# First batch of a forgetting-attention + MLP kernel on one core: unread matmuls out of its stream, block copies in halves ahead of the divisions, decay rows later, MLP steps among the last block's scores

## The chip, the cores and the metric

The kernel runs on one core of a Trainium2 chip. The engines of a core work through their own instruction streams and wait for each other by semaphores: PE (TensorE, matmuls; its weight loads are shown as PEld), DVE (VectorE), ACT (ScalarE), POOL (GpSimd) and SP (SyncE); the last two, and ACT, also issue DMAs. The metric is the time of the kernel on the device in microseconds (us); lower is better. Times inside a profile are counted from the start of its span.

## The reference

The inputs are q, k, v of 8 batches x 8 heads x 576 positions x 64, a forget gate f of 8 x 8 x 576, and two weights w_in (512 x 2048) and w_out (2048 x 512). The output is 4608 x 512, float32.

```python
scores = scale * np.matmul(q, k.transpose(0, 1, 3, 2))
log_f = np.log(np.clip(f, 0.0001, 1.0))
cum = np.cumsum(log_f, axis=-1)
decay = cum[:, :, :, None] - cum[:, :, None, :]
scores = np.where(causal, -1000000000.0, scores + decay)
attn = np.exp(scores - max); attn = attn / (sum + 1e-09)
x = matmul(attn, v), heads side by side: 4608 x 512
h = x @ w_in
g = h - np.tanh(h)
out = g @ w_out
```

## The kernel before

**Tiling.** The 576 positions of a head are four blocks of 128 and one of 64. The decay goes into the score matmul itself: next to their 64 channels, q and k carry three more rows (67 in all) that hold the cumulated log gate (as a high part `chi`, a low part `clo`, and `cq` for q) against rows of ones and minus ones. Scores are made transposed, keys on partitions; `exp` on ACT (L272 for the first batch, L329 for the others) writes them to fp16 tiles `e`; a second matmul with v, which carries a column of ones, gives values and row sums in a tile `av`; DVE divides (L285 to L287 for the first batch, L354 to L356 for the others) into `xn`. The divided values are turned into `XR`, a ring of four batches of x, transposed. The MLP runs over units `u` of 512 tokens: `mlp1` makes 128 rows of h for 512 tokens (for unit 0: two such for 256 tokens, L381), ACT takes tanh (L369), DVE adds (L371); `mlp2` multiplies with w_out. One MLP **step** is one `mlp1` tile or a quarter of an `mlp2` tile, about 0.87 us of PE at full clock.

**The order is written out by hand** (`manual_schedule`): every engine runs its instructions in the order of the Python calls, and waits in that order. From batch 1 on, `slot` interleaves one pair of heads (seven score tiles, the values of the pair before, transposes, loads) with a number of MLP steps, `TAKE` for the first six pairs and 8 for the rest. The change doesn't touch this part but for one number in `TAKE`.

**The first batch** is done before that, block by block, so that work can start when the first blocks of q and k have arrived:

- `load_first` and `load_v` (L90, L86) load blocks of q, k and v by POOL, `load_qk` batch 1's q and k, `load_win` w_in in two halves, `load_wout` w_out in four parts. A ring of eight semaphores lets the next load on POOL's queue start when the one eight places before it has landed.
- `decay_sum`, `decay_turn`, `decay_cols` sum the log gate (DVE, L153), transpose it (PE, L172, tile `ct`) and write it into the extra columns of q and k of the first batch (DVE, L177 to L180). `decay_rows` makes `chi`, `cq`, `clo` for all batches (DVE, L158 to L162); `load_aug(1)` puts them into batch 1's `QT` and `KT` by DMAs on SP (L148 to L150).
- `trans0(ib, what, pool, eng)` transposes block `ib` of q or k for all 8 heads (8 matmuls, L252) into one PSUM tile and copies it to `QT` or `KT` in one instruction (DVE L257, ACT L255).
- `scores0(ib, ti)` makes one tile of 512 columns of block `ib`'s scores (L267, with L270 for the mask on the diagonal) and its `exp`. Heads come in order, so a block's first tiles read the first heads alone. There are two PSUM tiles for scores and ten `e` tiles.
- `values0(ib)` makes the values of block `ib` and the division behind them. There is one `av` tile.
- `turn0(ib)` transposes `xn` on PE (L296) and copies it into `XR` (DVE L297).
- `spin(n)` issues n matmuls of ones with ones, 512 columns each (L223), into an `av` tile that nobody reads.

In the order before, a spin of 8 opens PE's stream, and seven more spins stand between the blocks' parts. A block's transposes and copies come after the division of the block two before it, and the first three MLP steps come after `scores0(4, 2)`, `scores0(4, 3)` and `scores0(4, 4)`.

Batch 1's q and k are loaded in another layout and transposed by `trans` (PE L234), whose result is copied in two parts, each by ACT (L241) or DVE (L243) as its last argument says ("AV", "VV").

Of the kernel before, what the change touches and what calls it, by code (L numbers as in the profile page):

```python
# [22 lines left out]
def kernel(  # L23
# [76 lines left out]
    def load_v(b, n):  # L100
        load_block(vn[b % 2], v, b, n)
# [65 lines left out]
    def decay_turn(blocks):  # L167
        if not CT:
            CT.append(ps_tr.tile([P, UW], FP32, tag="tr", name="ct"))
        for ib in blocks:  # L170
            t0 = min(ib * P, S - P)
            nc.tensor.transpose(out=CT[0][:, ib * H:(ib + 1) * H], in_=cum[0:H, t0:t0 + P], identity=id32)  # L172

    def decay_cols(b0, b1):
        ct = CT[0][:, b0 * H:b1 * H].rearrange("p (n h) -> p n h", h=H)
        hi = ka[:, b0:b1, :, D]
        nc.vector.tensor_scalar(out=qa[:, b0:b1, :, D + 2], in0=ct, scalar1=inv_qscale,  # L177
                                scalar2=-SHIFT * inv_qscale, op0=ALU.mult, op1=ALU.add)
        nc.vector.tensor_scalar_mul(out=hi, in0=ct, scalar1=inv_qscale)
        nc.vector.scalar_tensor_tensor(out=ka[:, b0:b1, :, D + 1], in0=ct, scalar=inv_qscale, in1=hi,  # L180
                                       op0=ALU.mult, op1=ALU.subtract)
# [36 lines left out]
    E, XN, GT, M2 = {}, {}, {}, {}  # L218

    def spin(n):  # L220
        av = ps_av.tile([P, 2, 512], FP32, tag="av", name="spin")
        for _ in range(n):
            nc.tensor.matmul(out=av[:, 0, :], lhsT=ones16[:, 0:P], rhs=ones16[:, 0:UW])  # L223

    def trans(b, c, src, dst, eng):
        pn, g3 = S // NT6, NT6 // 2
        if b == 1 and src is kn:
            t32 = ps_m.tile([P, UW], FP32, tag="m", name="t32")
        else:
            t32 = ps_tr.tile([P, UW], FP32, tag="tr", name="t32")  # L230
        t16 = t32.bitcast(FP16)[:, 0:2 * S // 2].rearrange("p (a g n) -> p a g n", a=2, g=g3)
        for a in range(2):
            for g in range(g3):
                nc.tensor.transpose(out=t16[:, a, g, :],  # L234
                                    in_=src[b % 2][:, 2 * c + a, 2 * g:2 * g + 2, :],
                                    identity=id16[0:pn, 0:pn])
        for e in range(2):
            to = dst[b % 2][0:D, 2 * c:2 * c + 2, e:S:2].rearrange("d a (p g) -> d a p g", g=g3)
            of = t16[e * D:(e + 1) * D, :, :, :].rearrange("d a g p -> d a p g")
            if eng[e] == "A":  # L240
                nc.scalar.activation(out=to, in_=of, func=AF.Copy)  # L241
            else:
                nc.vector.tensor_copy(out=to, in_=of)  # L243

    def trans0(ib, what, pool, eng):
        src, dst = (qa, ka)[what], (QT, KT)[what][0]
        p0 = max(0, (ib + 1) * P - S)
        pn = P - p0
        t32 = pool.tile([P, UW], FP32, tag="tr" if pool is ps_tr else "m", name="t32")
        t16 = t32.bitcast(FP16)[0:D + 3, 0:H * pn].rearrange("p (h n) -> p h n", h=H)  # L250
        for h in range(H):
            nc.tensor.transpose(out=t16[:, h, :], in_=src[p0:P, ib, h, 0:D + 3], identity=id16[p0:P, p0:P])  # L252
        to = dst[:, :, ib * P:ib * P + pn]
        if eng == "A":
            nc.scalar.activation(out=to, in_=t16, func=AF.Copy)  # L255
        else:
            nc.vector.tensor_copy(out=to, in_=t16)  # L257

    def scores0(ib, ti):
        w = min(P, S - ib * P)  # L260
        n = UW // w
        ps = ps_sc.tile([P, 512], FP32, tag="sc", name="ps")
        e = aex.tile([P, 512], FP16, tag="e", name="e")
        todo = [(h, j) for h in range(H) for j in range(ib + 1)][n * ti:n * ti + n]
        for i, (h, j) in enumerate(todo):
            at = slice(i * w, (i + 1) * w)
            nc.tensor.matmul(out=ps[:, at], lhsT=KT[0][:, h, j * P:(j + 1) * P],  # L267
                             rhs=QT[0][:, h, ib * P:ib * P + w], start=True, stop=(j < ib))
            if j == ib:
                nc.tensor.matmul(out=ps[:, at], lhsT=neg16, rhs=tri16[:, 0:w], start=False, stop=True)  # L270
            E[(0, h, j, ib)] = e[:, at]
        nc.scalar.activation(out=e, in_=ps, func=AF.Exp, scale=qscale)  # L272

    def values0(ib):
        w = min(P, S - ib * P)
        av = ps_av.tile([P, 2, 512], FP32, tag="av", name="av")
# [10 lines left out]
        nc.vector.tensor_tensor(out=XN[(0, ib)].rearrange("p (i c) (a d) -> p i (c a) d", i=2, a=2),  # L287
                                in0=av[:, :, :, 0:D], in1=rs.to_broadcast([w, 2, HH, D]), op=ALU.mult)
# [131 lines left out]
    def step(n=1):  # L420
        for fn, *args in mlp[done[0]:done[0] + n]:
            fn(*args)
        done[0] += n
# [29 lines left out]
        step(take - given)  # L453

    load_v(0, 0)
    spin(8)
    decay_sum(0, 2 * P)
    decay_turn((0, 1))
    decay_cols(0, 1)
    decay_sum(2 * P, S)  # L460
    trans0(0, 0, ps_m, "V")
    trans0(0, 1, ps_m, "A")
    decay_turn((2, 3, 4))
    decay_cols(2, NJ)
    load_first(qa, q, 2)
    load_first(ka, k, 2)
    load_v(0, 1)
    load_first(qa, q, 3)
    load_first(ka, k, 3)
    load_v(0, 2)  # L470
# [6 lines left out]
        load_qk(qn, q, 1, h, h + 2)  # L477
        load_qk(kn, k, 1, h, h + 2)
    load_win(DFF // 2, DFF)
    spin(2)  # L480
    decay_cols(1, 2)
    decay_rows(False)
    trans0(1, 0, ps_m, "V")
    scores0(0, 0)
    scores0(0, 1)
    trans0(1, 1, ps_tr, "V")
    decay_rows(True)
    load_aug(1)
    spin(2)
    scores0(1, 0)  # L490
    values0(0)
    scores0(1, 1)
    spin(1)
    trans0(2, 0, ps_m, "V")
    scores0(1, 2)
    trans0(2, 1, ps_tr, "V")
    scores0(1, 3)
    turn0(0)
    values0(1)
    spin(1)  # L500
    scores0(2, 0)
    scores0(2, 1)
    spin(1)
    trans0(3, 0, ps_m, "V")
    scores0(2, 2)
    turn0(1)
    scores0(2, 3)
    trans0(3, 1, ps_tr, "V")
    for e in EL:
        nc.vector.memset(e, 0.0)  # L510
    nc.vector.memset(KT[1][:, :, S:PITCH], 0.0)
    nc.vector.memset(vn[1][D:P, NJ - 1, :, 0:D], 0.0)
    nc.vector.memset(vn[1][:, :, :, D:VW], 1.0)
    for n in range(NJ):
# [5 lines left out]
    scores0(2, 4)  # L520
    scores0(2, 5)
    scores0(3, 0)
    values0(2)
    scores0(3, 1)
    scores0(3, 2)
    scores0(3, 3)
    turn0(2)
    trans0(4, 0, ps_m, "V")
    scores0(3, 4)
    trans0(4, 1, ps_tr, "V")  # L530
    scores0(3, 5)
    scores0(3, 6)
    scores0(3, 7)
    scores0(4, 0)
    values0(3)
    scores0(4, 1)
    scores0(4, 2)
    step()
    turn0(3)
    scores0(4, 3)  # L540
    step()
    scores0(4, 4)
    step()
    values0(4)
    trans(1, 0, qn, QT, "AV")
    step()
    trans(1, 0, kn, KT, "VV")
    step()
    TAKE = [4, 4, 3, 3, 10, 9]
# [33 lines left out]
```

## Time and profile before

| what | value |
|---|---|
| three runs | 364.15, 364.20, 362.62 us, median 364.15 |
| the profiled execution | 363.46 us, of which its span 361.8 us |
| L407, `mlp2` matmuls on PE | 576 of mean 378 ns, 140.2 us busy |
| L395, `mlp1` matmuls on PE, units 1 to 8 | 576 of mean 355 ns, 125.6 us busy |
| L272, `exp` of the first batch on ACT | 25 of mean 596 ns, 14.1 us busy |
| L223, spins on PE, up to 41 us | 15, 6.0 us busy |
| granted clock of PE, mean | 0.989 |
| DMA, whole span | 38.70 MB, mean 107 GB/s |

A matmul's duration in the rows includes time that it overlaps with its neighbours, so PE's work is better read from the distance of the starts: the eight matmuls of an `mlp1` step start 0.87 us before whatever follows them. In a timeline row, the brackets at the end hold how long the engine was idle before the instruction and what ended that wait. In the page's rows of 40 digits, each digit is the share of a slice of 9 us in tenths.

### The profile page before, as it was taken

How to read it: one execution, taken by the hardware profiler on the slowest of the kernel's cores; microseconds unless marked ns; L12 is line 12 of the kernel's file. 1: busy time of each engine (PE TensorE's matmuls, PEld its weight loads, DVE VectorE, ACT ScalarE, POOL GpSimd, SP SyncE). 2: the span in 40 equal slices, each digit the busy share in tenths (PEclk: the TensorE clock that was granted, in tenths of full speed). 3: DMA queues.
4: the chain of work that ended last, by engine and by line, in shares of the span. 5: the costliest groups of instructions: out<-in, count | busy, mean ns of one | idle time of the engine just before them, and what ended most of it. 6: DMA issues, size and time to landing. Idle time of an engine off the chain costs nothing.

```text
span 361.8 us, 7844 instructions
## 1 busy us (share of the span) xinstructions
PE 348.7 (96%) x2992; PEld 202.3 (56%) x2992; DVE 192.7 (53%) x358; ACT 223.5 (62%) x411; POOL 150.4 (42%) x288
## 2 busy tenths in 40 slices
PE   7789799999999999999999999999999999999995
PEld 3678687555555555555556875555555554444442
DVE  7653798546981478137823683277327612712810
ACT  5475687456765786568656875687568734613621
POOL 8944623256277626763676357642222210000000
PEclk9996999999999999999999999999999999999999
DMA  9999999999579997999699959991220022011002
GB/s 95 144 203 184 205 200 120 99 138 180 70 57 150 143 150 59 156 152 143 56 150 170 142 53 151 160 153 24 81 71 18 18 74 74 2 52 65 2 31 85
DMA packets 148439, 38.70 MB, mean 107 GB/s; under 512 B 137330, under 2 KB 142770, under 8 KB 148402
## 3 DMA queue, kind: packets, MB, share of 16 engines
q0 software_dynamic: 100128, 18.36, 69.3%
q1 hardware_dynamic: 48194, 19.77, 26.8%
q8 instruction: 23, 0.38, 0.4%
q14 instruction: 14, 0.11, 0.1%
q10 hardware_dynamic: 80, 0.08, 0.1%
HBM read 36.85 MB, written 9.44 MB: 128 GB/s over the span
## 4 chain that ended last, share of the span: by engine, by line
PE 91%; DVE 4%; ACT 3%; issue 1%; ACTq 0%
PE ops L407 34%; PE hps L395 30%; PE ps L320 10%; PE av L348 7%; PE hps L381 3%; PE ps L267 2%; PE spin L223 1%; DVE KT L243 1%; PE av L280 1%; PE t L252 1%; DVE gt L371 1%; PE t L234 1%; ACT e L329 1%; ACT th L369 1%; ACT e L272 1%
## 5 line engine op out<-in xcount | busy, mean ns | idle before, releaser
L407 PE MATMUL ops<-wout,gt 128*128 128x512 f16 x576 | 140.2, 378 | 0.0
L371 DVE TENSOR_TENSOR gt<-hps,th 128x512 f16<-128x512 f32 x144 | 99.1, 690 | 61.7 <-ACT th L369 60.9
L329 ACT ACTIVATE e<-ps 128x512 f16<-128x512 f32 x168 | 99.3, 594 | 49.2 <-PE ps L320 39.7
L395 PE MATMUL hps<-XR,win 128*128 128x512 f16 (+1 forms) x576 | 125.6, 355 | 0.2 <-DVE gt L371 0.2
L369 ACT ACTIVATE th<-hps 128x512 f32<-128x512 f32 x144 | 86.1, 598 | 28.8 <-PE hps L395 22.9
L339 POOL TENSOR_SCALAR_AFFINE_SELECT e<-e 128x128 f16<-128x128 f16 x144 | 49.0, 340 | 108.6 <-ACT e L329 108.2
L407 PEld LDWEIGHTS <-gt 128*128 128x128 f16 x576 | 51.8, 97 | 52.8
L395 PEld LDWEIGHTS <-win 128*128 128x128 f16 x576 | 52.3, 97 | 44.3 <-issue 0.5
L320 PE MATMUL ps<-QT,KT 67*128 67x512 f16 (+1 forms) x336 | 70.9, 277 | 3.0 <-DVE KT L243 2.0
L320 PEld LDWEIGHTS <-KT 67*128 67x128 f16 x336 | 32.8, 98 | 35.7 <-DVE KT L243 2.4
L411 ACT ACTIVATE ost<-ops 128x512 f32<-128x512 f32 x36 | 21.5, 598 | 39.2 <-PE ops L407 39.2
L354 DVE TENSOR_SCALAR rs<-av 128x10 f32<-128x10 f32 x28 | 4.6, 164 | 68.3 <-PE av L348 68.2
L86 POOL DMA_DIRECT2D vn<-in_v_dram x40 | 34.3, 859 | 13.1 <-DMA win<-in_moe_w_in_dram 5.1
L348 PEld LDWEIGHTS <-e 128*128 128x128 f16 x784 | 28.1, 97 | 5.5
L348 PE MATMUL av<-vn,e 128*128 128x65 f16 x784 | 29.1, 193 | 0.0
L86 POOL DMA_DIRECT2D qn<-in_q_dram x25 | 21.2, 850 | 9.8 <-PE t L234 3.6
L356 DVE TENSOR_TENSOR xn<-av,rs 128x640 f16<-128x640 f32 x28 | 23.1, 825 | 1.0
L86 POOL DMA_DIRECT2D kn<-in_k_dram x25 | 21.4, 855 | 1.4 <-issue 1.2
L272 ACT ACTIVATE e<-ps 128x512 f16<-128x512 f32 x25 | 14.1, 596 | 10.2 <-PE ps L270 5.4
L381 PE MATMUL hps<-XR,win 128*128 128x256 f16 x128 | 17.4, 281 | 0.0
L243 DVE COPY KT<-t 64x576 f16<-64x576 f16 x16 | 12.7, 796 | 1.9 <-PE t L234 1.8
L243 DVE COPY QT<-t 64x576 f16<-64x576 f16 x12 | 9.6, 803 | 7.5 <-PE t L234 5.2
(78 smaller groups left out, 210.6 us busy)
## 6 DMA issues: line engine op xcount, KB each, us to landing
out_dram<-ost SPq DMA_DIRECT2D x36, 256.0 KB
vn<-in_v_dram POOLq DMA_DIRECT2D x32, 128.0 KB, 5.2
qn<-in_q_dram POOLq DMA_DIRECT2D x24, 128.0 KB, 3.9
kn<-in_k_dram POOLq DMA_DIRECT2D x24, 128.0 KB, 4.1
win<-in_moe_w_in_dram POOLq DMA_DIRECT2D x2, 1024.0 KB, 12.9
wout<-in_moe_w_out_dram POOLq DMA_DIRECT2D x4, 512.0 KB, 12.2
XR<-xn SPq DMA_TRANSPOSE x56
qn<-in_q_dram POOLq DMA_DIRECT2D x1, 576.0 KB, 15.5
```

What stands on the lines that cost most here:

```text
L86: nc.gpsimd.dma_start(out=dst[0:pn, n, h0:h1, 0:D], in_=src[b, h0:h1, n * P:n * P + pn, :].rearrange("h p d -> p h d"))
L243: nc.vector.tensor_copy(out=to, in_=of)
L320: nc.tensor.matmul(out=ps[:, col:col + n], lhsT=KT[b % 2][0:D + 3, h, j * P:(j + 1) * P], rhs=QT[b % 2][0:D + 3, h, i0:i0 + n], start=True ...
L329: nc.scalar.activation(out=e[:, lo:hi], in_=ps[:, lo:hi], func=AF.Exp, scale=qscale)
L339: nc.gpsimd.affine_select(out=view, in_=view, compare_op=ALU.is_ge, fill=0.0, base=0, pattern=pat, channel_multiplier=-1)
L348: nc.tensor.matmul(out=av[:, a, ib, :], lhsT=E.pop((b, 2 * c + a, j, ib)), rhs=vn[b % 2][:, j, 2 * c + a, 0:D + 1], start=(j == 0), stop=( ...
L356: nc.vector.tensor_tensor(out=xn.rearrange("p i (a d) -> p a i d", a=2), in0=av[:, :, :, 0:D], in1=rs.to_broadcast([P, 2, NJ, D]), op=ALU. ...
L369: nc.scalar.activation(out=th, in_=hps, func=AF.Tanh, scale=-1.0)
L371: nc.vector.tensor_tensor(out=gt, in0=hps, in1=th, op=ALU.add)
L381: nc.tensor.matmul(out=hps[:, w * SB:(w + 1) * SB], lhsT=win[:, ci, ft * P:(ft + 1) * P], rhs=XR[:, ci, t * SB:(t + 1) * SB], start=(ci == ...
L395: nc.tensor.matmul(out=hps[:, o:o + n], lhsT=win[:, ci, s * P:(s + 1) * P], rhs=XR[:, ci, t:t + n], start=(ci == 0), stop=(ci == NCH - 1))
L407: nc.tensor.matmul(out=ops, lhsT=GT[(u, ft, m)], rhs=wout[:, ft, :], start=(ft == 0), stop=(ft == NFT - 1))
```

## The change

All of it is in the first batch. `trans0` is split into the transposes (`trans0`, for a range of heads) and the copy (`copy0`, for a range of heads), `values0` into the matmuls and the division (`norm0`), so that they can be ordered apart. `spin` is called with 8 at the start and with 2 behind the first block's transposes, and nowhere else. The rest is order: block 1 and block 2 are copied in halves of four heads; a block's copies are put ahead of the division of the block two before it; `decay_rows` is called between blocks 2 and 3 and between blocks 3 and 4, and `load_aug(1)` after that; v of block 1 is loaded ahead of q and k of block 2; memsets of batch 1's tiles move into the head on DVE, and those of the `el` tiles to POOL; `trans` of batch 1's first k uses ACT for one of its copies; a sixth MLP step is put ahead of the pairs and one is taken out of the second slot.

```diff
-    def trans0(ib, what, pool, eng):
-        src, dst = (qa, ka)[what], (QT, KT)[what][0]
+    T0 = {}
+
+    def trans0(ib, what, pool, h0=0, h1=H):
+        src = (qa, ka)[what]
...
-        to = dst[:, :, ib * P:ib * P + pn]
+    def copy0(ib, what, eng, h0=0, h1=H):
+        w = min(P, S - ib * P)
+        to = (QT, KT)[what][0][:, h0:h1, ib * P:ib * P + w]
         if eng == "A":
-            nc.scalar.activation(out=to, in_=t16, func=AF.Copy)
+            nc.scalar.activation(out=to, in_=T0[(ib, what)][:, h0:h1, :], func=AF.Copy)
         else:
-            nc.vector.tensor_copy(out=to, in_=t16)
+            nc.vector.tensor_copy(out=to, in_=T0[(ib, what)][:, h0:h1, :])
...
+        AV[ib] = av
+
+    def norm0(ib):
+        w = min(P, S - ib * P)
+        av = AV.pop(ib)
```

The order after, in full from the first load to the pairs:

```python
    load_v(0, 0)
    load_v(0, 1)
    spin(8)
    decay_sum(0, 2 * P)
    decay_turn((0, 1))
    nc.vector.memset(KT[1][:, :, S:PITCH], 0.0)
    nc.vector.memset(vn[1][D:P, NJ - 1, :, 0:D], 0.0)
    nc.vector.memset(vn[1][:, :, :, D:VW], 1.0)
    decay_cols(0, 1)
    trans0(0, 0, ps_m)
    trans0(0, 1, ps_m)
    copy0(0, 0, "V")
    copy0(0, 1, "A", 0, HH)
    copy0(0, 1, "A", HH, H)
    spin(2)
    decay_sum(2 * P, S)
    decay_cols(1, 2)
    scores0(0, 0)
    scores0(0, 1)
    decay_turn((2, 3, 4))
    for h in (0, HH):
        trans0(1, 0, ps_m, h, h + HH)
        trans0(1, 1, ps_m, h, h + HH)
    copy0(1, 0, "V", 0, HH)
    copy0(1, 1, "V", 0, HH)
    decay_cols(2, NJ)
    ...
    copy0(1, 0, "V", HH, H)
    copy0(1, 1, "V", HH, H)
    scores0(1, 0)
    scores0(1, 1)
    values0(0)
    trans0(2, 0, ps_m)
    scores0(1, 2)
    trans0(2, 1, ps_tr)
    scores0(1, 3)
    for h in (0, HH):
        copy0(2, 0, "V", h, h + HH)
        copy0(2, 1, "V", h, h + HH)
    scores0(2, 0)
    scores0(2, 1)
    norm0(0)
    trans0(3, 0, ps_m)
    copy0(3, 0, "V")
    scores0(2, 2)
    trans0(3, 1, ps_tr)
    copy0(3, 1, "V")
    scores0(2, 3)
    values0(1)
    norm0(1)
    scores0(2, 4)
    turn0(0)
    decay_rows(False)
    scores0(2, 5)
    scores0(3, 0)
    scores0(3, 1)
    trans0(4, 0, ps_m)
    copy0(4, 0, "V")
    scores0(3, 2)
    trans0(4, 1, ps_tr)
    copy0(4, 1, "V")
    scores0(3, 3)
    values0(2)
    norm0(2)
    scores0(3, 4)
    turn0(1)
    decay_rows(True)
    load_aug(1)
    load_v(1, 0)
    load_v(1, 1)
    for e in EL:
        nc.gpsimd.memset(e, 0.0)
    ...
    scores0(3, 5)
    scores0(3, 6)
    scores0(3, 7)
    scores0(4, 0)
    scores0(4, 1)
    values0(3)
    norm0(3)
    turn0(2)
    scores0(4, 2)
    step()
    scores0(4, 3)
    step()
    scores0(4, 4)
    turn0(3)
    step()
    values0(4)
    norm0(4)
    trans(1, 0, qn, QT, "AV")
    step()
    trans(1, 0, kn, KT, "AV")
    step()
    step()
    TAKE = [4, 3, 3, 3, 10, 9]
```

What the two lines of "..." leave out are loads in the order of before: q and k of blocks 2 and 3, v of blocks 2 and 3, q, k, v of block 4, the first half of w_in, batch 1's q and k of heads 0 to 3, the second half of w_in; and then v of batch 1's blocks 2 to 4, q and k of its heads 4 to 7, and w_out. The same part of the order before:

```python
    spin(2)
    decay_cols(1, 2)
    decay_rows(False)
    trans0(1, 0, ps_m, "V")
    scores0(0, 0)
    scores0(0, 1)
    trans0(1, 1, ps_tr, "V")
    decay_rows(True)
    load_aug(1)
    spin(2)
    scores0(1, 0)
    values0(0)
    scores0(1, 1)
    spin(1)
    trans0(2, 0, ps_m, "V")
    scores0(1, 2)
    trans0(2, 1, ps_tr, "V")
    scores0(1, 3)
    turn0(0)
    values0(1)
    spin(1)
    scores0(2, 0)
    scores0(2, 1)
    spin(1)
    trans0(3, 0, ps_m, "V")
    ...
    step()
    trans(1, 0, kn, KT, "VV")
    step()
    TAKE = [4, 4, 3, 3, 10, 9]
```

More of the change, by code (lines that the diff above doesn't have):

```diff
@@ L216 @@
                     LOADS.setdefault((p0 + 3, 2 * n + a), []).append(lambda b=b, dst=dst, src=src, a=a, c=c: place(dst, src, b, a, c))
-    E, XN, GT, M2 = {}, {}, {}, {}
+    E, XN, GT, M2, AV = {}, {}, {}, {}, {}
     def spin(n):
@@ L243, in trans @@
                 nc.vector.tensor_copy(out=to, in_=of)
-    def trans0(ib, what, pool, eng):
-        src, dst = (qa, ka)[what], (QT, KT)[what][0]
+    T0 = {}
+    def trans0(ib, what, pool, h0=0, h1=H):
+        src = (qa, ka)[what]
         p0 = max(0, (ib + 1) * P - S)
         pn = P - p0
[L249 to L252, printed above, removed]
-        to = dst[:, :, ib * P:ib * P + pn]
+        if (ib, what) not in T0:
+            t32 = pool.tile([P, UW], FP32, tag="tr" if pool is ps_tr else "m", name="t32")
+            T0[(ib, what)] = t32.bitcast(FP16)[0:D + 3, 0:H * pn].rearrange("p (h n) -> p h n", h=H)
+        for h in range(h0, h1):
+            nc.tensor.transpose(out=T0[(ib, what)][:, h, :], in_=src[p0:P, ib, h, 0:D + 3],
+                                identity=id16[p0:P, p0:P])
+    def copy0(ib, what, eng, h0=0, h1=H):
+        w = min(P, S - ib * P)
+        to = (QT, KT)[what][0][:, h0:h1, ib * P:ib * P + w]
         if eng == "A":
-            nc.scalar.activation(out=to, in_=t16, func=AF.Copy)
+            nc.scalar.activation(out=to, in_=T0[(ib, what)][:, h0:h1, :], func=AF.Copy)
         else:
-            nc.vector.tensor_copy(out=to, in_=t16)
+            nc.vector.tensor_copy(out=to, in_=T0[(ib, what)][:, h0:h1, :])
     def scores0(ib, ti):
@@ L455 @@
     load_v(0, 0)
+    load_v(0, 1)
     spin(8)
@@ L458 @@
     decay_turn((0, 1))
+    nc.vector.memset(KT[1][:, :, S:PITCH], 0.0)
+    nc.vector.memset(vn[1][D:P, NJ - 1, :, 0:D], 0.0)
+    nc.vector.memset(vn[1][:, :, :, D:VW], 1.0)
     decay_cols(0, 1)
+    trans0(0, 0, ps_m)
[3 more added lines that the diff above has]
+    copy0(0, 1, "A", HH, H)
+    spin(2)
     decay_sum(2 * P, S)
-    trans0(0, 0, ps_m, "V")
-    trans0(0, 1, ps_m, "A")
+    decay_cols(1, 2)
+    scores0(0, 0)
+    scores0(0, 1)
     decay_turn((2, 3, 4))
+    for h in (0, HH):
[3 more added lines that the diff above has]
+    copy0(1, 1, "V", 0, HH)
     decay_cols(2, NJ)
@@ L466 @@
     load_first(ka, k, 2)
-    load_v(0, 1)
     load_first(qa, q, 3)
@@ L479 @@
     load_win(DFF // 2, DFF)
-    spin(2)
-    decay_cols(1, 2)
-    decay_rows(False)
[L483 to L486, printed above, removed]
+    copy0(1, 0, "V", HH, H)
+    copy0(1, 1, "V", HH, H)
+    scores0(1, 0)
+    scores0(1, 1)
+    values0(0)
+    trans0(2, 0, ps_m)
+    scores0(1, 2)
+    trans0(2, 1, ps_tr)
+    scores0(1, 3)
+    for h in (0, HH):
+        copy0(2, 0, "V", h, h + HH)
+        copy0(2, 1, "V", h, h + HH)
+    scores0(2, 0)
+    scores0(2, 1)
+    norm0(0)
+    trans0(3, 0, ps_m)
+    copy0(3, 0, "V")
+    scores0(2, 2)
+    trans0(3, 1, ps_tr)
+    copy0(3, 1, "V")
+    scores0(2, 3)
+    values0(1)
+    norm0(1)
+    scores0(2, 4)
+    turn0(0)
+    decay_rows(False)
+    scores0(2, 5)
+    scores0(3, 0)
+    scores0(3, 1)
+    trans0(4, 0, ps_m)
+    copy0(4, 0, "V")
+    scores0(3, 2)
+    trans0(4, 1, ps_tr)
+    copy0(4, 1, "V")
+    scores0(3, 3)
+    values0(2)
+    norm0(2)
+    scores0(3, 4)
+    turn0(1)
     decay_rows(True)
     load_aug(1)
[L489 to L508, printed above, removed]
-    for e in EL:
[L510 to L514, printed above, removed]
+    load_v(1, 0)
+    load_v(1, 1)
+    for e in EL:
+        nc.gpsimd.memset(e, 0.0)
+    for n in range(2, NJ):
         load_v(1, n)
@@ L519 @@
         load_wout(t, t + 4)
[L520 to L530, printed above, removed]
     scores0(3, 5)
@@ L534 @@
     scores0(4, 0)
+    scores0(4, 1)
     values0(3)
-    scores0(4, 1)
+    norm0(3)
+    turn0(2)
     scores0(4, 2)
     step()
-    turn0(3)
     scores0(4, 3)
@@ L542 @@
     scores0(4, 4)
+    turn0(3)
     step()
     values0(4)
+    norm0(4)
     trans(1, 0, qn, QT, "AV")
     step()
-    trans(1, 0, kn, KT, "VV")
+    trans(1, 0, kn, KT, "AV")
     step()
-    TAKE = [4, 4, 3, 3, 10, 9]
+    step()
+    TAKE = [4, 3, 3, 3, 10, 9]
     for p in range(NPAIR, len(pairs) + 1):
```

## The prediction

> **What bounds the kernel now.** I read the page first, then its clock row, then the head in equal intervals, then the PE timeline and the DMA landings there.
>
> ```profile
> PE 348.7 (96%) x2992; PEld 202.3 (56%) x2992; DVE 192.7 (53%) x358; ACT 223.5 (62%) x411; POOL 150.4 (42%) x288
> ...
> PE   7789799999999999999999999999999999999995
> PEclk9996999999999999999999999999999999999999
> ```
>
> TensorE (PE) is full from the fifth slice (9 us each) to the end: what follows the head goes on PE's own time, so an edit in the head is worth what it moves the start of that dense stretch. The first four slices are not full, and in the fourth the granted clock is 0.6. The windows, cut at the moments where the clock changes:
>
> ```profile
> 12.20:15.62 3.42, 2.56 (x45) 2.33 (x45) 2.35 (x5) 1.75 (x3) 3.42 (x6) 1.00 2.26 150
> 15.62:19.03 3.41, 2.15 (x31) 1.81 (x32) 1.32 (x5) 1.09 (x2) 3.36 (x7) 1.00 1.49 153
> 19.03:22.44 3.41, 3.11 (x65) 2.92 (x63) 2.61 (x10) 2.79 (x5) 1.73 (x2) 1.00 1.11 201
> 22.44:25.86 3.42, 2.96 (x48) 2.42 (x46) 2.18 (x6) 2.51 (x5) 0.00 (x0) 1.00 1.29 207
> 25.86:29.27 3.41, 3.08 (x53) 2.99 (x51) 0.02 (x1) 1.94 (x4) 3.38 (x5) 0.50 1.13 209
> 29.27:32.68 3.41, 3.41 (x40) 2.88 (x38) 1.12 (x4) 1.68 (x3) 0.41 (x1) 0.50 1.92 172
> 32.68:36.09 3.41, 3.41 (x69) 3.03 (x67) 2.15 (x4) 2.28 (x4) 1.63 (x3) 1.00 1.92 178
> ```
>
> Columns: length, then busy time of PE, weight load, DVE, ACT, POOL, the granted clock, DMA share, GB/s. From 25.86 to 32.68 PE ran at half clock: 6.8 us that held some 3.4 us of full-speed work. The PE timeline has the waits and the first MLP steps:
>
> ```profile
> 13.00 0.39 PE L223 MATMUL spin<-ones 128*128 128x512 f16 x1 [0.88 <-DVE xn L287]
> ...
> 17.18 0.39 PE L223 MATMUL spin<-ones 128*128 128x512 f16 x1 [1.22 <-DVE xn L287]
> ...
> 30.04 1.89 PE L381 MATMUL hps<-XR,win 128*128 128x256 f16 x8
> ...
> 32.69 1.04 PE L381 MATMUL hps<-XR,win 128*128 128x256 f16 x8
> ...
> 40.61 0.39 PE L320 MATMUL ps<-QT,KT 67*128 67x512 f16 x1 [1.96 <-DVE KT L243]
> ```
>
> An unread matmul (spin) writes the tile `av`, so it waits for the division (L287) that reads the tile before, and all of PE stands behind it: 0.88 and 1.22 us. The first MLP step starts at 30.04 (1.7 us long at half clock, against 0.87 later), the second at 32.69. Batch 1's first scores wait 1.96 us for the two KT copies on DVE. PE's waits from 5.4 to 41 us add to 6.0 us (0.29, 0.26, 0.29, 0.88, 1.22, 0.30, 0.46, 0.33, 1.96).
>
> **Arrivals.** Issue plus time to landing, block by block, from the DMA view: q and k of block 2 land at 10.65 and 11.49, of block 3 at 13.64 and 14.53, of block 4 at 17.82 and 18.11; the first half of w_in (issued 14.81, 10.8 us) at 25.61, its second half at 33.06; batch 1's heads 4 to 7 at 39.4 (q) and 41.0 (k); batch 2's q and k at 54.2 and 57.6. The DMA row is full to about 90 us, so I take these as set by the DMA engines. The new order moves v of block 1 ahead of q and k of block 2: these come one place later (11.5 and 12.5, the landings of the next two places before). Every later load keeps its place.
>
> **Part by part.**
>
> Spins: five of the seven behind the first eight go, 5 x 0.216 = 1.1 us of PE, and with them the waits of 0.88 and 1.22.
>
> Head: copies of KT block 0 in two halves on ACT. One copy took 1.02 us (7.22 to 8.24); a half I take at 0.59, as the 512-element exponentials take, so the first four heads' scores can start at 7.8 instead of 8.74. Chi and cq (1.1 us of DVE) no longer precede block 1's copies; with the halves at 0.42 (the 512-element copies of block 4) block 1's first scores start at 10.4 instead of a wait that ended at 11.06. By then PE runs into block 2's arrival at 11.5, so little of this counts by itself. Three memsets (0.27, 0.27, 0.12) move into DVE's 0.83 us wait for `ct`: nothing, or 0.1 us if the wait shrinks.
>
> Blocks 2 to 4: the new order puts both transposes and their copies ahead of the division of two blocks earlier. Laid end to end by hand with the rows' pitches (a 128-column matmul 0.057 us, 8 transposes 0.46 to 0.5, an `av` matmul 0.03, a 1024-element copy 0.61, a half 0.36, a division 1.05, an exponential 0.49 in a row, 0.6 plus about 0.1 when waited for), I get block 2's first scores at 13.5 (17.40 before), block 3's at 17.0 (q, k 3 copied at 16.4), its eight exponentials done at 22.2, values of block 3 at 22.6, and scores0(4, 2) finished at 24.2. Of 17 exponentials between 14.0 and 24.9 that makes 0.64 us each; before, 15 took 10.3 us, 0.69. So the order is no faster than ACT and PE already show. The first MLP step then waits for w_in at 25.61: PE idles up to 1.4 us, which is also the slack for errors of mine. Chi, cq and clo (2.0 us of DVE) now stand among blocks 3 and 4, where DVE has 11 us of work in 13; the aug loads on SP follow at about 22 instead of 8.9 to 12.8 and need some 1 us (8.87 to 9.92 before): 10 us ahead of batch 1's scores. The three `el` memsets go to POOL, in front of a load that waits for w_in (5.1 us idle there): hidden; without that cover three POOL memsets delay that load by three times the 0.1 us of POOL's own small ones, or up to 0.35 for the three on DVE.
>
> MLP steps: step 1 at 25.65, scores0(4, 3) 0.37, step 2 at about 26.9. Before, step 2 started at 32.69, and the order from there to batch 1 is the same work. That is **-5.8 us**, half of it the half-clock stretch that step 1 no longer falls into.
>
> The 1.96 us gap: KT's second copy goes to ACT (0.80 beside 0.80) and a third step (0.87) is put before batch 1's scores, so I leave 0.3: **-1.7 us**. That step is taken out of a later slot, so it is cover and no gain.
>
> What is late next: all that follows would run 7.5 us earlier against loads that do not move. Batch 1's k heads 4 to 7 are first read at 51.13 - 7.5 = 43.6, after 41.0: fine. Batch 2's q is read at 61.13 - 7.5 = 53.6 (lands 54.2), k at 63.96 - 7.5 = 56.5 (lands 57.6): PE stalls about **+1.1 us**. For my hand schedule slipping past its slack I add **+0.5**.
>
> Sum: 363.46 (profiled execution, 361.8 of span and 1.66 around it) - 5.8 - 1.7 + 1.1 + 0.5 = 357.6. The median before is 0.7 above that execution, within a spread of 1.6; I forecast **357.8 us**.
>
> **The clock, the cost that the trace can't settle.** It fell at 25.86 after an interval in which PE was busy 2.96 of 3.42 us, and not after the one at 15.62 with 2.15 of 3.41 and a 1.22 us wait. Busy time does not decide. Adding up columns in the timeline, each weighted by its rows out of 128, transposes too, I get about 4900, 3750, 5140 and 2940 for the four intervals before the fall: the fall follows the poorest. My new order gives some 5400, 4500, 4400 and, with the wait for w_in, 3600 in the same intervals. So I expect the clock to hold, not by much. Bounds: nothing, or 3.4 us for two half-clock intervals of dense work as before.
>
> [...]
>
> **Rivals.**
>
> 1. The same order, but the clock falls around 25.9 as before, for two intervals under dense MLP steps: + 3.4, and batch 2's loads are then no longer late (- 1.1): 357.6 + 2.3 = about 360. For it: the interval from 22.44 stays the poorest. Against: steps fill it where nothing did.
>
> [...]
>
> 3. The change doesn't deliver: some in-order wait that I mislaid (a division in front of a copy, ACT behind a copy) keeps PE from reaching step 1 until about 30, and no clock is gained: only the 1.7 us at KT, less later stalls: 362.5 to 363.5. Against: every operand of step 1 but w_in is made by about 21, PE's own work from 9 to 24.2 is some 14 us by the pitches above, and so it takes 5 us of new waits. For it: those 14 us leave little room for any.
>
> **How the numbers follow.** Forecast 0.50, rival 1 0.26, rival 2 0.09, rival 3 0.15. A measurement of this kernel tells 0.5% (1.8 us): below 362.3 is faster, above 366.0 slower. Forecast, rival 1 and a third of rival 3 are faster: 0.81; the rest of rival 3 and a little of rival 2 same: 0.11; slower 0.08. The range runs from 355.6 (no slip, batch 2's loads a little earlier) through rival 1 and half of rival 3: 362.8.
>
> **What would show it.** Step 1's L393 row (L381 before) near 25.7 with a wait on the w_in DMA ahead of it; the clock in the windows from 12 to 36 at 1.00 (rival 1: 0.50 near 26 to 33; rival 2: 0.50 from before 20); block 2's scores near 13.5; no wait over 0.5 us at batch 1's first scores, at about 34; a new wait of up to 1 us of PE on batch 2's qn and kn loads near 54 to 57. I am wrong if step 1 starts after 28, or if the dense stretch starts early and PE then shows new waits further on that eat it.

## The result, and the profile after

| | median | runs | profiled execution | its span | mean granted clock |
|---|---|---|---|---|---|
| before | 364.17 us | 362.62 to 364.28 (4) | 363.46 us | 361.8 us | 0.989 |
| after | 357.77 us | 357.69 to 358.57 (4) | 358.57 us | 356.9 us | 1.000 |
| after, measured once more | 357.41 us | 357.28 to 357.56 (4) | 357.32 us | 355.6 us | 0.999 |

The change is faster: 0.9839 of the time before, 95% interval 0.9809 to 0.9869; in the second measurement 0.9825, 0.9806 to 0.9843. The forecast was 357.8 us. The two profiled executions of the same kernel differ by 1.3 us, and both are used below: the first is called "after", the other "after again".

The page of after, the lines that answer to those of before:

```profile
PE 346.6 (97%) x2987; PEld 200.9 (56%) x2987; DVE 191.9 (54%) x358; ACT 224.5 (63%) x413; POOL 150.9 (42%) x291
...
PE   7989998999999999999999999999999999999995
PEclk9999999999999999999999999999999999999999
```

PE is 80% busy or more from the second slice on, and the 0.6 of the fourth slice of the clock row is gone. The windows of after, in steps of 3.41 us from the clock's rise at 10.13 (length, busy time of PE, PEld, DVE, ACT and POOL, granted clock, DMA share, GB/s):

```profile
13.54:16.96 3.42, 3.25 (x54) 2.94 (x52) 2.55 (x9) 2.81 (x6) 3.42 (x6) 1.00 2.24 147
16.96:20.37 3.41, 3.11 (x61) 2.76 (x58) 3.26 (x8) 2.91 (x5) 3.15 (x5) 1.00 1.13 196
20.37:23.78 3.41, 3.17 (x68) 2.86 (x67) 2.54 (x7) 2.65 (x6) 1.86 (x5) 1.00 1.19 202
23.78:27.20 3.42, 3.04 (x76) 2.69 (x74) 1.32 (x5) 2.49 (x5) 2.52 (x4) 1.00 1.23 212
27.20:30.61 3.41, 3.41 (x49) 2.96 (x48) 2.39 (x5) 2.77 (x5) 0.67 (x1) 1.00 1.24 202
```

No interval is at 0.50; before, two were, from 25.86 to 32.68. The steps, in the PE timeline of after (start, duration, and in brackets the idle time before it and what ended it):

```profile
15.00 0.51 PE L274 MATMUL ps<-QT,KT 67*128 67x128 f16 x3
...
27.02 1.04 PE L393 MATMUL hps<-XR,win 128*128 128x256 f16 x8
...
28.20 1.04 PE L393 MATMUL hps<-XR,win 128*128 128x256 f16 x8
...
34.84 1.03 PE L393 MATMUL hps<-XR,win 128*128 128x256 f16 x8 [0.46 <-DVE gt L383]
35.71 0.38 PE L332 MATMUL ps<-QT,KT 67*128 67x512 f16 x1
...
38.18 0.19 PE L332 MATMUL ps<-QT,KT 67*128 67x64 f16 x1 [0.28 <-ACT e L341]
...
48.01 0.30 PE L332 MATMUL ps<-QT,KT 67*128 67x320 f16 x1 [0.62 <-ACT e L341]
...
54.75 0.30 PE L332 MATMUL ps<-QT,KT 67*128 67x320 f16 x1 [0.61 <-ACT e L341]
...
57.68 1.03 PE L419 MATMUL ops<-wout,gt 128*128 128x512 f16 x4
```

The rows of before that answer to the last two:

```profile
59.65 0.30 PE L320 MATMUL ps<-QT,KT 67*128 67x320 f16 x1 [0.61 <-ACT e L329]
...
62.58 1.03 PE L407 MATMUL ops<-wout,gt 128*128 128x512 f16 x4
```

Step 2 starts at 28.20 instead of 32.69, 4.49 us earlier, and batch 1's first scores at 35.71 instead of 40.61, 4.90 earlier, with six MLP steps done instead of five. The waits on the division (0.88 and 1.22) and on KT (1.96) are gone; in their place is a wait of 0.46 for `gt`. The rows behind that say what happened further on. Slots 1, 2 and 3 begin with their first scores at 35.71, 42.47 and 49.22, before at 40.61, 47.18 and 54.11. Slot 2 gave up a step of 0.87 us and has no other work for PE in its place: PE waits in it 0.62 us for ACT's exponentials (48.01), and the slot is only 0.18 us shorter than before (6.75 against 6.93). Slot 1 has as many steps as before and a new wait of 0.28 us (38.18): it is 0.19 us longer (6.76 against 6.57). The wait of 0.61 us in slot 3 was there before too, at 59.65. So the first `mlp2` step starts 4.90 us earlier than before (57.68 against 62.58), no more than batch 1's first scores did: the sixth step is not a gain there, and the span ends 4.9 us earlier.

In after again the same rows come earlier:

```profile
25.73 1.04 PE L393 MATMUL hps<-XR,win 128*128 128x256 f16 x8
...
26.91 0.82 PE L393 MATMUL hps<-XR,win 128*128 128x256 f16 x6
```

(The second row is cut by the end of the view.) In all 14 profiles PE starts at half its later pace: the spins of 512 columns start 0.43 us apart at first, and 0.22 us once the clock has risen. In after the clock rose at 10.13 us, in after again at 6.66, in the profile of before at 5.38; the 1.3 us between the two executions are there by block 2's first scores (15.00 and 13.70), and with the early rise step 2 stands at the 26.9 that was forecast.

### The profile page after: what moved, and what is told of

Read it like the earlier page. It is cut to its first block, busy times and chain, and to the rows that moved or that the text cites. A ratio compares the mean times of both kernels' runs of the same rounds, so it can differ in the third digit from the quotient of the medians.

```text
span 356.9 us, 7839 instructions
## 1 busy us (share of the span) xinstructions
PE 346.6 (97%) x2987; PEld 200.9 (56%) x2987; DVE 191.9 (54%) x358; ACT 224.5 (63%) x413; POOL 150.9 (42%) x291
## 4 chain that ended last, share of the span: by engine, by line
PE 92%; ACT 3%; DVE 2%; DMA 1%; issue 1%; ACTq 0%
PE ops L419 35%; PE hps L407 30%; PE ps L332 10%; PE av L360 7%; PE hps L393 3%; PE ps L274 2%; PE t L255 1%; PE av L287 1%; PE t L234 1%; ACT e L279 1%; ACT th L381 1%; ACT e L341 1%; DVE gt L383 1%; DMA lf<-in_f_dram 1%; PE ps L277 1%
## 5 line engine op out<-in xcount | busy, mean ns | idle before, releaser
L341 ACT ACTIVATE e<-ps 128x512 f16<-128x512 f32 x168 | 99.2, 594 | 47.4 <-PE ps L332 40.0
L393 PE MATMUL hps<-XR,win 128*128 128x256 f16 x128 | 16.6, 272 | 0.5 <-DVE gt L383 0.5
L274 PE MATMUL ps<-QT,KT 67*128 67x128 f16 (+1 forms) x120 | 11.6, 214 | 1.5 <-ACT e L279 0.8
```

What stands on the lines that cost most here:

```text
L341: nc.scalar.activation(out=e[:, lo:hi], in_=ps[:, lo:hi], func=AF.Exp, scale=qscale)
L393: nc.tensor.matmul(out=hps[:, w * SB:(w + 1) * SB], lhsT=win[:, ci, ft * P:(ft + 1) * P], rhs=XR[:, ci, t * SB:(t + 1) * SB], start=(ci == ...
```

## The experiments

Three questions: did the clock hold because the stream got denser, or for another reason; which part of the change brought the time; and what the prediction's misses cost. Each kernel was timed against the kernel before on the same chip: medians there 363.95 (19 runs), 363.55 (13) and 363.97 us (7).

### Which of it is the spins, and which the clock

**old_fill**: before, with six unread matmuls more among block 3's scores.

```diff
+    def fill(n):
+        t = ps_m.tile([P, UW], FP32, tag="m", name="fill")
+        for _ in range(n):
+            nc.tensor.matmul(out=t, lhsT=ones16[:, 0:P], rhs=ones16[:, 0:UW])
...
     scores0(3, 1)
+    fill(1)
```

and one more behind each of `scores0(3, 2)` to `scores0(3, 6)`.

> The old order with six more unread matmuls of 512 columns among block 3's scores, in the stretch 22.4 to 25.9 us ahead of the fall of the clock; they write a PSUM tile of the MLP pool that no engine reads, so they wait for no division. Theory that the clock falls after an interval with too few columns: the clock stays at 1.00 from its first rise to 41 us, the first MLP step starts near 28 instead of 30.0, and the time falls by 1.5 to 2.5 us although 1.3 us of PE work is added. [...]

Measured: 362.23 us (361.64 to 363.27, 10 runs), ratio 0.9963 [0.9944, 0.9982]; the profiled execution kept full clock from 7.29 to the end, with step 1 at 29.56 (not near 28, as expected) and step 2 at 30.96. Its clock row:

```profile
PEclk9999999999999999999999999999999999999999
```

More work on the engine that bounds the kernel, six matmuls of 0.216 us, made the kernel 1.7 us shorter. The waits behind the spins and the 1.96 us at KT are still in its timeline. The clock did not hold in every run: five of the ten have a mean clock of 0.998 or 0.999 and took 361.6 to 361.9 us, the other five have 0.993 to 0.995 and took 362.6 to 363.3; where it fell in these is not known. Of the 19 runs of before beside them, two have 0.999 (361.5 us), three 0.994 or 0.995, and fourteen 0.989 or 0.990 (363.7 to 364.2). The fill is the only edit, so the work in the stretch ahead of 25.86 bears on the fall: with the six matmuls five of ten runs have 0.998 or more, without them two of 19. Before's own runs at 0.999 and at 0.989 or 0.990 are some 2 to 3 us apart.

**old_no_spin**: before, without its five later spins.

```diff
     load_aug(1)
-    spin(2)
     scores0(1, 0)
...
     scores0(1, 1)
-    spin(1)
     trans0(2, 0, ps_m, "V")
...
     values0(1)
-    spin(1)
     scores0(2, 0)
     scores0(2, 1)
-    spin(1)
     trans0(3, 0, ps_m, "V")
```

> The old order with the change's spins only (8 at the start and 2 behind block 0's transposes; five later ones gone), nothing else. Theory that the spins cost by their wait for a division: PE's waits of 0.88 and 1.22 us shrink, the stretch to the first MLP step gets up to 2 us shorter, and the time falls by 0.5 to 2 us unless the clock falls more. Rival, that the spins hold the clock: the half clock comes before 20 us and lasts longer than 6.8 us, and the time rises by 1 to 4 us.

Measured: 359.63 us (359.2 to 361.1, 4 runs), ratio 0.9896 [0.9856, 0.9936]. Deleting five matmuls from the old order, with whole copies, early decay rows and the old tail, brings 4.3 us of the change's 6.4, more than twice what was expected. Step 1 starts at 26.04, step 2 at 27.45, and the clock holds near 25.9. It falls later, at the wait for KT, as the windows of old_no_spin show:

```profile
28.72:32.14 3.42, 3.42 (x66) 3.01 (x62) 2.42 (x6) 2.19 (x4) 0.00 (x0) 1.00 1.78 179
32.14:35.55 3.41, 1.44 (x17) 1.03 (x15) 3.24 (x6) 1.30 (x3) 2.58 (x4) 1.00 2.06 175
35.55:38.96 3.41, 3.41 (x22) 2.48 (x21) 1.30 (x2) 1.96 (x4) 2.68 (x4) 0.50 1.29 205
```

The interval with 1.44 us of busy PE holds the wait:

```profile
35.38 0.48 PE L320 MATMUL ps<-QT,KT 67*128 67x512 f16 x1 [1.97 <-DVE KT L243]
```

Here the wait of about 2 us lies whole in one interval, and the interval after it, dense work, runs at half clock. In before the wait of 1.96 us was shared by two intervals (cut at 39.51) and the clock held. So the same wait cost 1.96 us before and more than that here.

**new_spin**: the change, with one spin put back behind each of the divisions of blocks 0 and 1.

```diff
     norm0(0)
+    spin(1)
...
     norm0(1)
+    spin(1)
```

> The new order with one unread matmul into the av tile right behind each of the first two divisions, so that PE waits for these divisions again. Theory that the order is worth its time because PE no longer stands behind a division: PE waits some 0.8 to 1.2 us at each, the first MLP step moves from 27.0 to about 28.5, and the time rises by 1 to 2 us. Rival, that the gain is the clock alone: the time stays within 0.5 us, as the clock stays at 1.00.

Measured: 360.29 us (359.95 to 363.77, 10 runs), ratio 0.9922 [0.9891, 0.9952]: eight runs at 360.0 to 360.4 with a clock near 1.0, two at 363.7 with 0.986. The profiled execution was one of the two; its timeline has the old waits back, one of 0.74 and one of

```profile
19.37 0.39 PE L223 MATMUL spin<-ones 128*128 128x512 f16 x1 [1.22 <-DVE xn L299]
```

and its windows the old fall:

```profile
18.29:21.70 3.41, 2.02 (x26) 1.59 (x26) 2.35 (x6) 1.53 (x4) 2.87 (x6) 1.00 1.12 210
21.70:25.12 3.42, 3.42 (x47) 3.07 (x46) 0.97 (x3) 1.99 (x4) 2.10 (x3) 0.50 1.28 200
```

Two unread matmuls of together 0.43 us cost 2.5 us with their waits (360.3 against 357.8) and 6 us where the clock falls as well (363.7). The price of a spin here is not its length but the division it waits for.

### Which of it is the tail, and which the order

**old_nospin_tail**: old_no_spin with the change's tail alone.

```diff
-    trans(1, 0, kn, KT, "VV")
+    trans(1, 0, kn, KT, "AV")
     step()
-    TAKE = [4, 4, 3, 3, 10, 9]
+    step()
+    TAKE = [4, 3, 3, 3, 10, 9]
```

> The old order without its five later spins, and with the change's tail: batch 1's first k copied by ACT and DVE side by side, a sixth step ahead of the pairs, TAKE of the change. Nothing else of the new order (old division order, whole copies, rows early). Theory now, after the old order without spins gave 359.63: the spins and this tail are nearly all of the change, and the gap of 1.97 us ahead of batch 1 and the half-clock interval behind it go: 357.2 to 358.2, within 0.5 us of the new order. Rival (the prediction's): copies ahead of divisions, halves and later rows bring some 2 us of their own: 359 to 360.

Measured: 357.64 us (357.6 to 359.28, 4 runs), ratio 0.9851 [0.9813, 0.989], clock 1.0. That is the change's own time (357.77 and 357.41), without its block order, its halves, its late decay rows and its moved memsets. In the medians, whatever these bring is not told apart from nothing. What they may bring is a margin for the clock: one of the four runs here fell to 0.995 (359.28 us), and one of old_nospin_take below to 0.994, where all sixteen runs of the change, new_take and new_best have 0.998 or more. So few runs do not show it. Step 1 starts at 26.07 here and at 25.73 in after again.

**new_vv**: the change with the old tail (`"VV"`, five steps, the old `TAKE`).

> The new order with the old tail: batch 1's first k copied twice by DVE, five steps ahead of the pairs, TAKE of before. By the prediction's term, 1.2 to 1.7 us slower than the new order. Theory now: PE waits about 2 us for DVE ahead of batch 1 instead of 0.46, but the step left in slot 2 covers the exponentials there: + 0.6 to + 1.0, unless the wait makes an interval too poor and the clock falls for one interval, then up to + 2.5.

Measured: 358.47 us (357.73 to 359.11, 4 runs), ratio 0.9862 [0.982, 0.9904]: 0.7 to 1.1 us behind the change. The wait of 1.97 us for KT is back, and the step that was its cover is back in slot 2, where it costs next to nothing. So the tail is worth 2.0 us in the old order, where the wait also cost an interval of clock, and 1.1 at the most in the new one, where the clock of the profiled execution held (its interval from 31.85 has 3504 columns by the weighted count of the last section, against 2676 in old_no_spin).

**new_norm_first**: the change with the divisions of blocks 0 and 1, and the values of block 1, back ahead of the copies of blocks 2 and 3.

```diff
     values0(0)
+    norm0(0)
     trans0(2, 0, ps_m)
...
     scores0(2, 0)
+    values0(1)
+    norm0(1)
     scores0(2, 1)
-    norm0(0)
     trans0(3, 0, ps_m)
...
     scores0(2, 3)
-    values0(1)
-    norm0(1)
```

> The new order with the first two divisions back ahead of the copies of the block two later. Theory that copies ahead of divisions matter: block 2's and 3's scores start 0.5 to 1 us later each, the first MLP step comes about 1 us later, + 0.5 to + 1.2 us. Rival, that PE's own work and the exponentials set the pace there: within 0.3 us of the new order.

Measured: 358.46 us (357.31 to 360.14, 4 runs), ratio 0.9866 [0.9822, 0.9911]. The profiled execution, 357.31, has step 1 at 25.75 and equals after again (357.32, 25.73). The other three runs are 0.7 to 2.8 us longer, one with a clock of 0.995; the median is 0.7 to 1.0 us behind the change, as the theory had it, but four runs so far apart do not say whether the order costs anything. Unclear; in the median it is less than the 2.5 us that two spins behind these divisions cost in new_spin.

**new_rows_early**: the change with `decay_rows` and `load_aug(1)` put back behind the decay columns.

```diff
     decay_cols(2, NJ)
+    decay_rows(False)
+    decay_rows(True)
+    load_aug(1)
...
     turn0(0)
-    decay_rows(False)
...
     turn0(1)
-    decay_rows(True)
-    load_aug(1)
```

> The new order with all decay rows and the loads of batch 1's rows back early, behind decay_cols(2, 5). Theory that 2.0 us of DVE in front of block 1's second halves are on the path: scores0(1, 2) 1 us later, + 0.5 to + 1.2 us. Rival, that the arrival of block 2 hides them: within 0.3 us. The first half of w_in landed at 25.6 in the old order with these loads early and at 22.7 to 23.7 in three of the later runs: if the small loads were the cause it lands late again here.

Measured: 361.14 us (359.01 to 362.4, 10 runs), ratio 0.9943 [0.9917, 0.9968]. The timeline shows the wait, block 1's scores of heads 4 to 7 behind the second half of its copies:

```profile
13.98 0.56 PE L274 MATMUL ps<-QT,KT 67*128 67x128 f16 x2 [1.40 <-DVE QT L264]
```

and the windows what follows it:

```profile
12.68:16.09 3.41, 1.99 (x25) 1.55 (x26) 2.74 (x8) 1.09 (x2) 3.41 (x6) 1.00 2.32 154
16.09:19.50 3.41, 3.26 (x31) 3.25 (x31) 2.08 (x6) 1.82 (x4) 2.97 (x5) 0.50 1.29 160
```

The one run with a clock of 1.0 took 359.01, 1.2 to 1.6 us over the change, about the wait; the others, at 0.989 to 0.993, add the clock. So the place of the rows on DVE matters in the new order, and yet old_nospin_tail, with the rows early, is as fast as the change: there `chi` and `cq` stand ahead of block 1's copies and `clo` behind them, and here all three stand in one piece between the two halves of these copies. Whether the rows' small loads delay w_in was a second question here: its first half landed at 24.90, and at 22.7 to 24.4 in the other experiments, those with early rows among them. That is too little to say so.

### What was left

**new_take**: the change with another number of steps per slot.

```diff
-    TAKE = [4, 3, 3, 3, 10, 9]
+    TAKE = [4, 4, 3, 3, 9, 9]
```

> The new order with TAKE = [4, 4, 3, 3, 9, 9]: the sixth step ahead of the pairs is taken out of the fifth slot, where mlp2 fills PE, and no longer out of the second slot. Theory that the step taken out of slot 2 left PE waiting for the exponentials (waits of 0.62 and 0.61 us at 48.0 and 54.8 against one of 0.61 before): 0.6 to 0.9 us faster than the new order, so 6.8 to 7.4 us below the old. Rival, that ACT's rate sets these slots whatever PE has: the same as the new order within 0.3 us.

Measured: 356.60 us (356.43 to 356.91, 4 runs), ratio 0.9806 [0.9772, 0.9841], about 1 us below the change. Slot 2 has its step back and slot 5 gives one up. PE's waits on `e` (L341) from 8 to 62 us add to 1.3 us instead of 1.9: the one of 0.62 in slot 2 is gone, and no new one has come. With the sixth step ahead of the pairs, the step is better taken from the later slot.

**old_nospin_gapfill**: old_no_spin with four unread matmuls ahead of the pairs, where PE waits for KT.

```diff
     step()
+    spin(4)
```

> The old order without its five later spins, with four unread matmuls of 512 columns put where PE waits 1.97 us for DVE ahead of batch 1 (32.4 to 35.4 us). Theory that the clock falls behind an interval of 3.41 us with fewer than about 3000 row-weighted columns (2676 there in the run without them, 4700 now): the clock stays at 1.00, and the time falls by 1.3 to 1.8 us from 359.6, to about 358, though the work is more. Rival, that the fall at 35.6 comes from the wait itself: the half-clock interval stays and the time is 359.6 or above.

Measured: 358.79 us (357.77 to 359.59, 4 runs), ratio 0.9861 [0.9833, 0.9889], against 359.63 for old_no_spin. The clock stays at 1.00 to the end of the profiled execution, and the wait splits:

```profile
33.26 1.03 PE L223 MATMUL spin<-ones 128*128 128x512 f16 x4
...
35.39 0.39 PE L320 MATMUL ps<-QT,KT 67*128 67x512 f16 x1 [1.10 <-DVE KT L243]
```

Batch 1's first scores start when they did (35.39 against 35.38), and the work behind them runs at full clock: 1.4 us less in the profiled spans (356.5 against 357.9), 0.8 in the medians, whose ranges overlap. Two of the four runs have a clock of 1.0 and took 357.8 and 358.3; the other two have 0.995 and took 359.3 and 359.6, so the clock did not always hold. The same instruction, two of which cost new_spin 2.5 us, pays in the profiled execution here, where it waits for nothing and stands where PE would be idle.

**old_nospin_take**: old_nospin_tail with the `TAKE` of new_take.

> The old order without its five later spins, with the change's tail, and TAKE = [4, 4, 3, 3, 9, 9]. Theory that the block order of the change is worth nothing once the spins are gone: 356.4 to 357.0, equal to the new order with the same TAKE (356.6). Rival, that the block order is worth something in a kernel with this TAKE: 0.5 us or more above 356.6.

Measured: 357.31 us (356.87 to 358.67, 4 runs), ratio 0.9828 [0.9801, 0.9855]. Of the 1 us that the same number brought in the new order, 0.3 appears in the old one, less than expected; one of the runs had a clock of 0.994. Its profiled execution (357.31) shows a wait that no other profile has: batch 2's k landed at 58.59 instead of 55.85 in new_take, and PE waited 0.69 us for it at 58.63. Up to there the two stand level (first `mlp2` step at 53.86 and 53.87). So most of the 0.9 us between these two executions is that landing; whether the block order brings it about, and whether the new order is 0.7 us better at its best, is open.

**after_again**: the change once more, beside the two above and the next.

> The changed kernel itself once more, beside the next three on the same chip: 357.5 to 358.6.

Measured: 357.41 us, as in the first table, just below what was expected.

**new_best**: new_take with the three memsets of batch 1's tiles taken out of the head again, to behind `load_aug(1)`.

> The new order with TAKE = [4, 4, 3, 3, 9, 9] and the three memsets of batch 1's tiles moved out of the head, behind the loads of batch 1's rows. In the trace of the new order they stand in DVE's chain (0.27, 0.27 and 0.12 us behind the first sum) and PE waits 0.48 us for the columns behind them, against 0.29. Theory that they are on the path: 0.2 to 0.4 us below 356.6. Rival, that PE's wait is for the transposed sums (ct) in any case: equal to 356.6 within 0.15.

Measured: 356.68 us (356.51 to 357.04, 4 runs), ratio 0.9803 [0.9781, 0.9825]: the time of new_take, so the rival held and not the theory. The memsets are hidden, as the prediction had it; PE's wait at the first transposes is 0.29 us in new_take and 0.28 in new_best. All runs of new_take and new_best are below all runs of before and after.

## Why the prediction was right, and where not

The sign, the total and the main mechanism were right: PE no longer stands behind the divisions, the MLP steps start earlier, and the clock does not fall under them. The total is also right by luck, because two errors took each other's place: the later steps were put 1.3 us too good, and 1.6 us were charged that did not come.

- **The spins.** Right: the waits of 0.88 and 1.22 us left with them, and putting two back brought them back (new_spin). Deleting the five is two thirds of the gain by itself.
- **Step 2 at 26.9, -5.8 us.** Mis-sized in the profiled execution: 28.20, -4.49. In after again it is 26.91, -5.78. The difference is the clock's first rise (10.13 against 6.66), of which the prediction had no term: it took the head's work at full clock from 5.4 on, as in the one execution that it had.
- **"The first MLP step then waits for w_in at 25.61."** Failed. The half landed at 22.89, and at 22.7 to 24.9 in all the other profiles but that of before; step 1 waited for a DMA in none of them. It starts when PE and ACT are through with the blocks, at 25.6 to 26.3 in the nine profiles without later spins where the clock rose before 8 us and held up to step 1. That the number came out at 25.7 all the same is chance: the hand schedule slipped (block 3's first scores came at 17.97 in after again, not at 17.0), and no idle time of "up to 1.4 us" was there behind it.
- **The order of the blocks.** The prediction laid it out at length and costed all of it into the 26.9. Half right: block 2's first scores were to start at 13.5 and did at about 13.7 in after again (15.00 in after). But the old order without its spins reaches step 1 at 25.59 to 26.07 (four profiles), the new one at 25.62 to 26.32 (five, but for after itself with its late rise). The clock rose earlier in those four (4.83 to 5.47) than in these five (6.43 to 7.96), but that does not hide a gain of the new order: new_spin, which is the new order up to block 2, rose at 4.64 and has block 2's first scores at 13.79, after again, with its rise at 6.66, at 13.70. What the hand schedule took for the new order's doing was the spins' undoing.
- **The gap at KT, -1.7.** The gap went as forecast, 1.96 to 0.46. The step that failed is "That step is taken out of a later slot, so it is cover and no gain", with nothing charged for the slot: cover is free only if the slot it is taken from has something else to fill it. PE waited 0.9 us more for ACT (0.62 in that slot and 0.28 in the one ahead of it), so the tail gave 0.4 us of the 1.7 (from -4.49 at step 2 to -4.90 at the first `mlp2` step). new_take bears it out: another slot, 1 us. The other 0.4 us went ahead of batch 1's scores: the gap left 0.46 us and not 0.3, and "the order from there to batch 1 is the same work" was not so, since `turn0(3)`, 0.22 us, now stands behind step 2 (29.38) and stood ahead of it before (31.73).
- **Batch 2's loads, +1.1.** Did not come in the change. The loads kept their places, as forecast (q landed at 54.09, k at 57.47, against 54.2 and 57.6), but they are read 4.90 us earlier and not 7.5 (56.23 and 59.06). In after again k landed at 57.68 and was read at 57.78: the limit was 0.1 us away, and its place was right: in the profile of old_nospin_take PE did wait there, 0.69 us.
- **The clock.** "I expect the clock to hold, not by much" was right. The forecast had 3600 columns for the poorest interval; counted the same way, after has 4308 at the least between 10.13 and 27.20, and after again 3266, while the four falls came after 2468 to 2937 (below). No wait of PE before these falls is over 1.97 us. Rival 1 did not come. The chances give 0.09 to rival 2, a half clock from before 20 us. No run shows that the missing spins bring it: the clock of after is 1.00 from 10.13 on, that of old_no_spin from 11.66 to 35.55; the one profile without later spins that is at 0.50 there, new_rows_early from 16.09, has the wait of 1.40 us ahead of it. Rival 3's new in-order wait came in new_rows_early and not in the change.

In the terms of the sum: -5.8 and -0.4 make 357.3 from 363.46, and after again took 357.32.

## What to carry to other kernels

Put unread matmuls where PE would be idle and into a tile that nothing reads or holds: four such left the clock at 1.00 in the profiled execution of old_nospin_gapfill and took 0.8 us off the median. The same ones in a tile that another engine still reads turn that engine's work into PE's wait: in new_spin two of them, 0.43 us, cost 2.5 us, and in two of its ten runs (363.7 us, clock 0.986) the clock fell as well. Before an order is redrawn, try the change without the redrawing: here five deletions and a tail of four lines gave the time of the whole, as far as four runs tell. When work is pulled forward as cover, read what the slot that gives it up will wait for.

## What the runs showed of the hardware

**The intervals ahead of a fall.** In before the granted clock was 1.00 from 5.38 for 20.48 us, 0.50 for 6.83 and 1.00 for 327.68; in after it was 1.00 from 10.13 for 348.16: 6, 2, 96 and 102 times 3.41 us. The windows of old_no_spin, new_spin and new_rows_early, taken in the same steps, are each at 1.00 or at 0.50. I counted, from the timelines, the columns that PE's matmuls and transposes started in each such interval, each weighted by its rows out of 128; a dense interval has about 7000. The falls of the four profiles that have one ahead of the end follow intervals with 2468 (new_rows_early), 2676 (old_no_spin), 2736 (new_spin) and 2937 (before). Every other full-clock interval counted, up to 345 us in before and after and up to 33 us in the other twelve profiles, has 2998 (new_norm_first, from 16.67) or more, and the clock held. PE's busy time does not separate them: it fell after 2.96 us of 3.42 (before, from 22.44) and held after 2.15 of 3.41 (before, from 15.62). Nor do columns without the weight (4608 fell in before, 4608 held in new_norm_first). Nor does the longest wait: the fall in before came after none over 1.22 us, and the clock held there through the wait of 1.96 us that ended at 40.61. The count was found after the fact, 2937 and 2998 lie close, and a few matmul records can be missing: it separates these intervals and shows neither a limit nor that the chip counts just this. It does not order the first rise: after 2561 columns at half pace the clock rose in new_best (from 3.63) and did not in after (from 3.30).

**With and without transposes.** Without them the count does not separate: the interval from 32.14 in old_no_spin has 2316 weighted columns that are no transposes and the clock fell (2676 with them), that from 10.13 in after has 1958 and it held (4520 with them). No run tested transposes alone.

**Where the intervals begin.** Counted back from the first rise (4.64 us in new_spin to 10.13 in after) in steps of 3.41 us, the intervals of the 14 profiles begin anywhere from 0.22 (new_best) to 3.30 us (after). So a wait is divided differently from one profile to the next: PE's wait of 1.97 us lies whole in one interval of old_no_spin, and that of 1.96 us in before is shared by two. (After and after again begin nearly alike, at 3.30 and 3.25; there the rise came one interval later in after.) The kernel before itself took 361.5 to 364.2 us in one set of runs, at 361.5 with a granted clock of 0.999 and at about 364 with 0.989; only one of its executions was profiled, so whether this is the reason is not shown. The change, whose thinnest intervals have 4308 and 3266 in its two profiles, ranges less (357.28 to 358.57 over eight runs).
